# Tokens kept once, in bf16, inside the residual rows; the last chunk's middle gelu tiles in the probabilities' buffer

## The chip, the cores and the metric

The kernel runs on one core of a Trainium2 chip. Five engines work beside each other and meet at semaphores: TensorE (PE, with its weight loads PEld), VectorE (DVE), ScalarE (ACT), GpSimd (POOL) and SyncE (SP, which here only issues DMAs). The metric is the device time of one execution in microseconds; times are medians of several runs.

## The reference

Two layers, each an attention block with a window of 256 tokens and an MLP, over 2048 tokens of width 576. Inputs, weights and output are bf16; both layers use the same weights.

```
def A(x):                       # 32 heads of 18
    q, k, v = (x @ wqkv)        # each [32, 2048, 18]
    s = q @ k.T * 18 ** -0.5    # where 0 <= i - j < 256, else -1e9
    return softmax(s) @ v @ wo
def B(x):
    return gelu(layernorm(x) @ w1 + b1) @ w2 + b2     # 576 -> 4608 -> 576

for layer in range(2):
    x = x + A(layernorm(x))
    x = x + B(layernorm(x))
```

## The kernel before

**Tiles and chunks.** The 2048 tokens are 16 tiles of 128, handled in chunks of four tiles. There are 8 chunks: 0 to 3 are layer one, 4 to 7 layer two (`CH`, `NK`). The residual `x_res` stays in SBUF as float32, one row of 576 per token and tile.

**The stages of a chunk k.** `qkv` (L807, for the first two chunks L767) makes q, k and v; q and k go through `qn` and a DMA transpose (L847) into `qT` and `kT`. `E` is attention, 8 groups of four heads in three parts, `ea`, `eb`, `ec`. In it `scores` (L874) makes the scores of one unit, ACT takes exponentials into `pT` (L883), POOL masks the edges of the window (L904), and `pv` (L921) multiplies with v. DVE normalises (L932 to L942). `tail` (stage `t`) multiplies with wo (L767), adds to the residual (`resid`, L981), takes statistics, and writes the normalised tile through a DMA transpose (L731) into `xnTm`. The MLP goes in three thirds of 12 hidden tiles: `G_part` (stages `ga`, `gb`, `gc`; L1027, 108 matmuls) with gelu on ACT (L1036) into `hT`, and `mm2` (stages `ma`, `mb`, `mc`; L1064, 96 matmuls) with w2, added to the residual, or in the last third of layer two to the output rows (L984).

**One buffer for all thirds.** `hT` holds one third, so the first gelu of a third waits until the product of the third before has read it. In the middle of the kernel the attention of the next chunk stands between the two. For the last chunk there is no next chunk, and the order is G, product, G, product, G, product. The product's first unit of six matmuls reads gelu tiles 0 to 5, all others read all 12. The gelu tiles of a third come in the order 0, 3, 1, 4, 2, 5, 6, 9, 7, 10, 8, 11 (`PAIRS`).

**Where the tokens lie.** Tiles 0 to 11 come in bf16 into the space of w2 (`x_in = w2_sb`), which is free then; the layer norms of chunks 0 to 2 and the first residual add of chunk 0 read them there. The first two w2 loads wait for gelu tiles of chunk 0 for that reason (`gate`). Tiles 4 to 15 are loaded by POOL with a cast to float32 into `x_res` (`x_load`). Parts of `x_res` that are not yet needed hold the transposed q (`qx`) and k (`kx`) of chunk 1.

**What sets the order.** Each step is given to `PL.add` with its engine, what it reads and writes, a cost and a priority. `PL.schedule` then plans all steps with these costs and writes a fixed order for each engine; steps wait for each other by semaphores (`Sched.add`). `PL.nudge` shifts the priority by stage; its numbers were searched for. `Bank` objects get one of the eight PSUM banks when the planner places them: attention scores take three pairs (0, 2, 4), `mm2` takes 7, 6, 5 or 4 (`FILL`), `G_part` any. Filler matmuls (L669) are put into gaps in the first 140 us of the plan. TensorE's array is used in four shapes: full, two halves of 64 rows (L807, L1027), four strips of 32 rows (L874) and four strips of 32 columns (L921).

**The queues.** All weight loads, token loads and transposes are issued by SP, in the planned order; POOL's queue has the three casting loads.

Of the kernel before, what the change touches and what calls it, by code (L numbers as in the profile page):

```python
# [40 lines left out]
class Sched:  # L41
# [23 lines left out]
    def add(self, eng, fn, reads=(), writes=(), dma=None, ring=4, own=False):  # L65
# [11 lines left out]
        for w in writes:  # L77
            for rd in self.readers.get(w, ()):
                if rd[2] != eng or rd[3]:
                    want(rd[:3])  # L80
            lw = self.last_write.get(w)
            if lw is not None and (own or not (eng == "pe" and lw[2] == "pe")):
                want(lw)
# [334 lines left out]
def build_kernel(nc, A_x, A_wqkv, A_wo, B_x, B_w1, B_b1, B_w2, B_b2, out):  # L418
# [42 lines left out]
    PL.nudge = {"": -172.82, "b": -56.78, "ea0.0": 8.44, "ea0.2": 25.12, "ea0.p0": 0.04, "ea0.p1": 10.45, "ea0.p2": -176.5,  # L461
# [120 lines left out]

    x_dram = A_x[0]
    out_dram = out[0]
    x_in = w2_sb

    def mm_cost(n):
        return max(n / 2400.0, 0.026) + (0.003 if n > 64 else 0.0)
# [670 lines left out]
```

## Time and profile before

| what | us |
|---|---|
| median of 3 runs | 888.36 (888.0 to 889.36) |
| the profiled execution | 886.86 |
| its span in the profile | 885.1 |
| PE, ACT, DVE, POOL busy | 860.2, 594.3, 418.8, 369.4 |
| granted TensorE clock | 1.00 |

The profile is one execution. Busy time is that of an engine's instructions, without what only waits or issues DMAs. A wait in a timeline stands in brackets behind the instruction before which the engine was idle, with what ended it. The timelines merge equal instructions that follow each other. Tile names have lost their digits: `w_sb` is `w1_sb` or `w2_sb`, so `w_sb<-in_A_x_dram` are the bf16 tokens. `q2.1`, `ga0` and the like are stages of the plan and appear in no profile.

### The profile page before, as it was taken

To read this page: it belongs to the slowest core of one execution; us is meant where nothing else is said; L and a number is where in the kernel's file an instruction comes from. 1 tells how busy PE (TensorE), PEld (TensorE's weight loads), DVE (VectorE), ACT (ScalarE), POOL (GpSimd) and SP (SyncE) were. 2 spreads that over 40 slices of the span, in tenths; PEclk is the share of its full clock that TensorE was granted. 3 is DMA by queue.
4 is the path that set the end of the run, shared out by engine and by line. 5 is a ranking of instruction groups with operands and counts; after the bars stand their busy time and mean duration, and the time that the engine had idled before them with its cause. 6 is when DMAs were issued, how large, how long until landed. Compare 5 with 4: busy or idle time off the path is not lost.

```text
span 885.1 us, 23132 instructions
## 1 busy us (share of the span) xinstructions
PE 860.2 (97%) x9679; PEld 508.5 (57%) x9679; DVE 418.8 (47%) x994; ACT 594.3 (67%) x741; POOL 369.4 (42%) x503
## 2 busy tenths in 40 slices
PE   9888999999999999999999999999999899999998
PEld 7445555555565556665566655555556455556655
DVE  6889324684337543763347632374325533262111
ACT  5874797778748596466772869747686769853332
POOL 3775464375235561325431446416344356222000
PEclk9999999999999999999999999999999999999999
DMA  7698625852493523864448342595435743347330
GB/s 191 125 191 162 181 89 156 231 129 73 161 177 104 161 83 117 180 150 147 108 126 182 68 161 84 142 191 115 137 123 147 166 138 110 117 124 208 129 119 30
DMA packets 182903, 122.48 MB, mean 138 GB/s; under 512 B 107472, under 2 KB 181264, under 8 KB 182800
## 3 DMA queue, kind: packets, MB, share of 16 engines
q1 hardware_dynamic: 181216, 117.46, 50.9%
q0 software_dynamic: 1584, 3.54, 1.4%
q8 instruction: 77, 1.26, 0.6%
q14 instruction: 26, 0.21, 0.1%
HBM read 91.28 MB, written 2.36 MB: 106 GB/s over the span
## 4 chain that ended last, share of the span: by engine, by line
PE 81%; DVE 4%; POOL 4%; DMA 3%; ACT 3%; issue 3%; SPq 1%; ACTq 0%; DVEq 0%; POOLq 0%
PE ps L1027 31%; PE ps L1064 29%; PE ps L807 7%; PE ps L874 5%; PE ps L921 4%; PE ps L767 4%; POOL pT L904 3%; ACT pT L883 2%; ACT hT L1036 1%; DVE xn L707 1%; DMA xnTm<-xn 1%; DMA xnTa<-xn 1%; DVE xn L715 1%; DVE st_all L682 1%; SPq L614 1%
## 5 line engine op out<-in xcount | busy, mean ns | idle before, releaser
L904 POOL TENSOR_SCALAR_AFFINE_SELECT pT<-pT 128x512 bf16<-128x512 bf16 (+1 forms) x368 | 286.8, 804 | 258.4 <-ACT pT L883 255.2
L883 ACT ACTIVATE pT<-ps 128x1024 bf16<-128x1024 f32 (+2 forms) x384 | 346.2, 972 | 54.1 <-PE ps L874 53.5
L1036 ACT ACTIVATE hT<-ps,b1col 128x512 bf16<-128x512 f32 x288 | 175.2, 688 | 213.0 <-PE ps L1027 212.7
L1064 PE MATMUL ps<-w_sb,hT 128*128 128x288 bf16 x2304 | 309.6, 287 | 3.3 <-ACT hT L1036 2.6
L1027 PE MATMUL ps<-xnTm,w_sb 64*128 64x512 bf16 x2592 | 291.4, 376 | 0.9 <-DMA xnTm<-xn 0.5
L1064 PEld LDWEIGHTS ps<-w_sb,hT 128*128 128x128 bf16 x2304 | 212.7, 98 | 86.0 <-issue 22.8
L1027 PEld LDWEIGHTS ps<-xnTm,w_sb 64*128 64x128 bf16 x2592 | 127.3, 94 | 143.5 <-issue 7.2
L981 DVE TENSOR_TENSOR x_res<-ps,x_res 128x288 f32<-128x288 f32 x216 | 95.6, 446 | 160.8 <-PE ps L1064 140.5
L932 DVE STREAM_TRANSPOSE oq<-ps 128x512 f32<-128x512 f32 x64 | 45.7, 714 | 134.9 <-PE ps L921 134.7
L807 PE MATMUL ps<-wqkv,xnTa 64*128 64x288 bf16 x1296 | 93.7, 283 | 4.2 <-DMA xnTa<-xn 2.0
L828 DVE CAST qn<-ps 128x288 bf16<-128x288 f32 x120 | 49.4, 449 | 79.2 <-PE ps L807 72.6
L807 PEld LDWEIGHTS ps<-wqkv,xnTa 64*128 64x128 bf16 x1296 | 60.4, 94 | 36.0 <-issue 4.5
L874 PE MATMUL ps<-qT,kT 32*128 32x384 bf16 (+2 forms) x1216 | 64.0, 276 | 4.1 <-ACT pT L883 3.7
L695 POOL TENSOR_SCALAR vtmp<-mv_all 128x1 f32<-128x1 f32 (+1 forms) x43 | 8.6, 201 | 133.6 <-DVE mv_all L686 132.4
L1042 POOL TENSOR_TENSOR x_res<-x_res,b2bc 128x576 f32<-128x576 f32 x32 | 40.4, 1283 | 51.8 <-ACT hT L1036 51.7
L921 PE MATMUL ps<-pT,vA 128*20 128x384 bf16 (+2 forms) x1408 | 50.7, 276 | 2.0 <-POOL pT L904 1.5
L874 PEld LDWEIGHTS ps<-qT,kT 32*128 32x128 bf16 x1216 | 19.4, 92 | 45.0 <-issue 28.1
L682 DVE BATCH_NORM_STATS2 st_all<-x_res 128x6 f32<-128x288 f32 x104 | 44.0, 441 | 0.8
L767 PE MATMUL ps<-wo_sb,attT 128*128 128x288 bf16 x320 | 42.1, 286 | 0.7 <-DVE x_res L981 0.6
L815 DVE CAST vA<-ps 128x288 bf16<-128x288 f32 x64 | 26.7, 451 | 34.1 <-PE ps L807 32.0
L707 DVE TENSOR_SCALAR xn<-x_res,mv_all,rstd 128x576 bf16<-128x576 f32 x52 | 36.1, 695 | 9.6 <-DMA xnTm<-xn 5.7
L921 PEld LDWEIGHTS ps<-pT,vA 128*20 128x20 bf16 x1408 | 25.6, 90 | 24.5 <-issue 12.1
(49 smaller groups left out, 388.6 us busy)
## 6 DMA issues: line engine op xcount, KB each, us to landing
w_sb<-in_B_w_dram SPq DMA_DIRECT2D x48, 864.0 KB, 5.7
w_sb<-in_B_w_dram SPq DMA_DIRECT2D x48, 768.0 KB, 4.7
w_sb<-in_B_w_dram SPq DMA_DIRECT2D x96, 48.0 KB, 4.4
x_res<-in_A_x_dram POOLq DMA_DIRECT2D x3, 1152.0 KB, 6.4
out_dram<-xn SPq DMA_DIRECT2D x16, 144.0 KB, 2.0
wqkv<-in_A_wqkv_dram SPq DMA_DIRECT2D x3, 576.0 KB, 5.3
w_sb<-in_A_x_dram SPq DMA_DIRECT2D x2, 576.0 KB, 4.8
wo_sb<-in_A_wo_dram SPq DMA_DIRECT2D x4, 144.0 KB, 2.9
```

The costliest lines, as they stand in the source:

```text
L682: add("dve", lambda e, i=i, s=s: e.bn_stats(st_all[:, t, i, :], s[:, t, i * HB:(i + 1) * HB]), reads=res, writes=[f"st{t}_{i}"], cost=0.37 ...
L767: ins = e.matmul(bank(bs[o])[:, 0:HB], lhs(c), rhs(c, o * HB), start=(c == 0), stop=(c == KD - 1))
L807: ins = e.matmul(bank(bs[o])[:, 0:HB], xnTa[r:r + 64, c, i * 128:(i + 1) * 128], wqkv[r:r + 64, c, col:col + HB], start=(c == 4), stop=(ph ...
L828: add("dve", lambda e, b=bs[o], dst=dst: e.tensor_copy(dst, heads_of(bank(b))), reads=[bs[o]], writes=[f"qn{sl}h{o}"], cost=0.375, lat=0.1 ...
L874: ins = e.matmul(two(bs[j // 2])[:, j % 2, col:col + nq * 128], k_of(T0 + so)[0][32 * j:32 * j + 32, g, :], qs[32 * j:32 * j + 32, g, qo * ...
L883: add("act", lambda e, h2=h2: e.activation(pT[:, sl, 2 * h2:2 * h2 + 2, lo:hi], two(bs[h2])[:, :, lo:hi], ACT.Exp, scale=SCALE), reads=[bs ...
L904: add("pool", lambda e, ap=ap, pat=pat, sgn=sgn, kind=kind: e.affine_select(ap, ap, pattern=pat, compare_op=(ALU.is_ge if kind == "d" else ...
L921: ins = e.matmul(bank(bo)[32 * j:32 * j + VW, qo * 128:(qo + nq) * 128], vA[:, (T0 + so) % VS, 8 * j + g, :], pT[:, sl, j, col:col + nq * ...
L981: add("dve", lambda e: e.tensor_tensor(x_res[:, t, sl], bank(b)[:, 0:HB], x_old[:, t, sl], ALU.add), reads=[b] + ([f"xin{t}"] if first els ...
L1027: ins = e.matmul(bank(bks[i])[:, 0:n], w1_sb[r:r + 64, sls[i], col:col + 128], xnTm[r:r + 64, k % 2, c, 0:n], start=(c == 4), stop=(ph == ...
L1036: add("act", lambda e, ff=ff, fl=fl, bk=bk: e.activation(hT[:, fl, 0:n], bank(bk)[:, 0:n], ACT.Gelu_apprx_tanh, bias=b1col[:, ff:ff + 1]), ...
L1064: ins = e.matmul(bank(b)[:, 0:HB], hT[:, fl, i * 128:(i + 1) * 128], w2_sb[:, fl, hh * HB:(hh + 1) * HB], start=(fl == 0), stop=(fl == NFH ...
```

## The change

1. The tokens are loaded once, in bf16, by SP. `x_in` is now the upper half of the float32 row itself: columns 288 to 575 of `x_res`, seen as 576 bf16 values. Tiles 12 to 15 have a load of their own, and POOL's casting loads are gone. All of layer one's first residual adds, statistics and first layer norms read these bf16 tokens. The add of the upper half (`hh == 1`) overwrites them, so it waits for DVE's own earlier reads of the same row (`own`).
2. The first two w2 loads no longer need the tokens' space: they wait for the first chunk's attention groups 5 and 7 (`aq5`, `aq7`) in place of gelu tiles 0 and 6.
3. `qx` moves into the lower halves of `x_res` rows 8 to 15, `kx` into `xnTm`.
4. The last chunk's middle third writes its gelu tiles into `pT` (`h_of`), which is free after its attention.
5. In the last chunk `mm2` may take any bank not held by `G_part`, and the units of its first two tiles that use gelu tiles 0 to 5 no longer wait for 6 to 11.
6. All numbers of `PL.nudge` are new.

```
-                if rd[2] != eng or rd[3]:
+                if own or rd[2] != eng or rd[3]:
...
-    PL.nudge = {"": -172.82, "b": -56.78, "ea0.0": 8.44, "ea0.2": 25.12, "ea0.p0": 0.04, "ea0.p1": 10.45, "ea0.p2": -176.5,
+    PL.nudge = {"": -255.24, "b": -219.8, "ea0.0": 23.65, "ea0.1": -0.79, "ea0.2": 6.45, "ea0.p0": -38.42, "ea0.p1": 20.22,
...
-    x_in = w2_sb
+    low = x_res[:, :, 0:HB].bitcast(BF16)
+    x_in = x_res[:, :, HB:D].bitcast(BF16)
...
-    qx = x_res[:, 12:16, :].rearrange("p t d -> p (t d)").bitcast(BF16)[:, 0:G * 512].rearrange("p (g c) -> p g c", g=G)
-    kx = x_res[:, 8:12, :].rearrange("p t d -> p (t d)").bitcast(BF16)[:, 0:2 * G * 128].rearrange("p (s g c) -> p s g c", s=2, g=G)
+    qx = low[:, 8:16, 0:512]
+    kx = xnTm[:, 1, 0:4, :].rearrange("p c (a q) -> p (c a) q", a=4).rearrange("p (s g) q -> p s g q", s=2)
...
-    def x_load(a, cnt, reads, prio):
-
-        dma("pool", x_res[:, a:a + cnt, :], x_dram[a * P:(a + cnt) * P, :].rearrange("(t p) d -> p t d", p=P), reads=reads,
-            writes=[r for t in range(a, a + cnt) for r in X(t)] + {8: ["kx0", "kx1"], 12: [f"qx{i}" for i in range(4)]}.get(a, []), cls="xr", ring=8, cost=1.2, prio=prio)
...
-                reads=[f"h{WB * b}"] if gate else [], writes=[f"w2s{b}"] + [f"xin{WB * b + i}" for i in range(WB if gate else 0)], cls="w2", ring=NFH // WB, cost=0.55, lat=2.0, move=0.44 * WB,
+                reads=[gate[b]] if gate else [], writes=[f"w2s{b}"], cls="w2", ring=NFH // WB, cost=0.55, lat=2.0, move=0.44 * WB,
...
+            over = []
+            if first:
+                over = [f"xin{t}"] if hh else [f"qx{i}" for i in range(4)] if t >= 8 else []
             add("dve", lambda e: e.tensor_tensor(x_res[:, t, sl], bank(b)[:, 0:HB], x_old[:, t, sl], ALU.add),
-                reads=[b] + ([f"xin{t}"] if first else []), writes=[f"x{t}h{hh}"], cost=0.375, lat=0.14, prio=prio)
+                reads=[b] + ([f"xin{t}"] if first else []), writes=[f"x{t}h{hh}"] + over, cost=0.375, lat=0.14, prio=prio, own=first and hh == 1)
...
-                resid(t, o, bs[o], prio, first=(k == 0))
+                resid(t, o, bs[o], prio, first=(l == 0))
...
+    hP = pT.rearrange("p s j c -> p (s j) c")
+
+    def h_of(k, hf, fl):
+        if k == NK - 1 and hf == 1:
+            return hP[:, fl, :], f"hp{fl}"
+        return hT[:, fl, :], f"h{fl}"
...
-                b = Bank(FILL)
+                b = Bank(FILL if k < NK - 1 else FILL + (3, 2, 1, 0))
...
-                    add("pe", fn, reads=[f"h{fl}" for fl in range(f0, f0 + 6 if f0 or i + hh == 0 else NFH)] + [f"w2s{f0 // WB}"], writes=[b],
+                    add("pe", fn, reads=[h_of(k, hf, fl)[1] for fl in range(f0, f0 + 6 if f0 or i + hh == 0 or k == NK - 1 and i < 2 else NFH)] + [f"w2s{f0 // WB}"], writes=[b],
...
-            ln_norm_T(t, i, xnTa, "xa", prio, dup=True)
+            ln_norm_T(t, i, xnTa, "xa", prio, None if l else x_in, None if l else [f"xin{t}"], dup=True)
...
-            ln_stats(t, 4 * k - 5)
+            ln_stats(t, 4 * k - 5, x_in, [f"xin{t}"])
...
-            w2_load(0, 1, True)
+            w2_load(0, 1, ("aq5", "aq7"))
...
-                x_load(CH[1][1], CH[1][2], ["aq7"], 0)
+                xin_load(12, 4, ["aq7"], 0)
```

More of the change, by code (lines that the diff above doesn't have):

```diff
@@ L731, in ln_norm_T @@
         add("sp", lambda e: e.dma_start_transpose(dst[:, :, i * 128:(i + 1) * 128], xn[:, sl, :]),
-            reads=rd, writes=[f"{dname}{i}"], dma="t", ring=8, cost=1.3, lat=0.6, move=0.72, desc=640, prio=prio)
+            reads=rd, writes=[f"{dname}{i}"] + (["kx0", "kx1"] if dname == "xm1_" else []), dma="t", ring=8, cost=1.3, lat=0.6, move=0.72, desc=640, prio=prio)
     w1n = [0]
@@ L750, in w1_load, with w2_load @@
                 lat=1.4, move=0.17, desc=64, prio=prio)
-    def w2_load(hf, prio, gate=False):
+    def w2_load(hf, prio, gate=None):
         for b in range(NFH // WB):
@@ L1032, in G_part @@
                         lat=0.22, alloc=(bb if ph == 0 else ()), fifo="pa", own=(ph == 1),
-                        after=([f"h{fs[i] - f}" for i in ix] if ph == 0 else ()))
+                        after=([h_of(k, hf, fs[i] - f)[1] for i in ix] if ph == 0 else ()))
             for ff, bk in zip(fs, bks):
                 fl = ff - f
-                add("act", lambda e, ff=ff, fl=fl, bk=bk: e.activation(hT[:, fl, 0:n], bank(bk)[:, 0:n], ACT.Gelu_apprx_tanh,
+                hd, hn = h_of(k, hf, fl)
+                add("act", lambda e, ff=ff, hd=hd, bk=bk: e.activation(hd[:, 0:n], bank(bk)[:, 0:n], ACT.Gelu_apprx_tanh,
                                                                       bias=b1col[:, ff:ff + 1]),
-                    reads=[bk, "b1"], writes=[f"h{fl}"], cost=0.145 + n * 0.00087, lat=0.17,
+                    reads=[bk, "b1"], writes=[hn] + ([f"p{fl // 4}{x}" for x in ("h0", "h1", "m0", "m1", "m2")] if hn[1] == "p" else []), cost=0.145 + n * 0.00087, lat=0.17,
                     fifo="act", prio=prio)
@@ L1063, in fn @@
                         for fl in range(f0, f0 + 6):
-                            ins = e.matmul(bank(b)[:, 0:HB], hT[:, fl, i * 128:(i + 1) * 128], w2_sb[:, fl, hh * HB:(hh + 1) * HB],
+                            ins = e.matmul(bank(b)[:, 0:HB], h_of(k, hf, fl)[0][:, i * 128:(i + 1) * 128], w2_sb[:, fl, hh * HB:(hh + 1) * HB],
                                            start=(fl == 0), stop=(fl == NFH - 1))
                         return ins
-                    add("pe", fn, reads=[f"h{fl}" for fl in range(f0, f0 + 6 if f0 or i + hh == 0 else NFH)] + [f"w2s{f0 // WB}"], writes=[b],
+                    add("pe", fn, reads=[h_of(k, hf, fl)[1] for fl in range(f0, f0 + 6 if f0 or i + hh == 0 or k == NK - 1 and i < 2 else NFH)] + [f"w2s{f0 // WB}"], writes=[b],
                         cost=6 * mm_cost(HB), lat=0.22, prio=prio + 0.05 * i, alloc=((b,) if f0 == 0 else ()),
@@ L1182, in build_kernel @@
                 w1_load(-1, ["aq6"])
-                x_load(CH[1][1], CH[1][2], ["aq7"], 0)
+                xin_load(12, 4, ["aq7"], 0)
             if k == 1:
                 for n, kk in enumerate(later):
-                    x_load(CH[kk][1], CH[kk][2], [], b + 2)
                     if kk > 2:
```

144 rows, old and new, of the table add are left out of this document.

## The prediction

> **What bounds the kernel now.** I read the page first: its head, the busy time and the chain that ended last.
>
> ```profile
> span 885.1 us, 23132 instructions
> PE 860.2 (97%) x9679; PEld 508.5 (57%) x9679; DVE 418.8 (47%) x994; ACT 594.3 (67%) x741; POOL 369.4 (42%) x503
> ...
> PE 81%; DVE 4%; POOL 4%; DMA 3%; ACT 3%; issue 3%; SPq 1%; ACTq 0%; DVEq 0%; POOLq 0%
> ```
>
> TensorE is busy for 860.2 of 885.1 us and makes up 81% of the chain; no other engine comes above 67%. So an edit can win in two ways only: fewer or cheaper steps on TensorE, or shorter waits of TensorE, of which there are 885.1 - 860.2 = 24.9 us. Then I asked where these lie, by windows: the first attention stage up to 57 us, the stretch up to the first gelu stage, the steady middle, and the last chunk's MLP.
>
> ```profile
> 0.00:57.00 57.00, 49.39 (x524) 31.17 (x524) 43.28 (x112) 42.22 (x63) 33.72 (x60) 1.00 0.72 166
> 57.00:93.40 36.40, 32.59 (x463) 18.84 (x461) 31.92 (x78) 19.98 (x23) 20.99 (x31) 1.00 0.76 153
> 93.40:820.00 726.60, 718.56 (x8195) 420.56 (x8196) 332.66 (x782) 509.54 (x625) 314.67 (x414) 1.00 0.53 140
> 820.00:885.10 65.10, 59.62 (x504) 37.94 (x503) 10.99 (x24) 22.53 (x32) 0.00 (x0) 1.00 0.28 92
> ```
>
> The columns are the stretch, its length, and the busy time of PE, PEld, DVE, ACT and POOL, then the granted clock, the DMA share and GB/s. The clock is 1.00 throughout, so it is no term. TensorE stands still for 7.6, 3.8, 8.0 and 5.5 us. What it waits for in the middle, from the table of waits of that window:
>
> ```profile
> PE ps L807 <- DMA xnTa<-xn: 2.0, 2, 1.4
> PE ps L874 <- ACT pT L883: 1.7, 2, 1.2
> PE ps L921 <- POOL pT L904: 0.7, 1, 0.7
> ...
> PE ps L1027 <- DMA xnTm<-xn: 0.5, 1, 0.5
> ```
>
> Few waits, each at another place: they come from the order in which the planner put the steps. The end is different, as the timeline of PE shows:
>
> ```profile
> 795.29 0.79 PE L767 MATMUL ps<-wo_sb,attT 128*128 128x288 bf16 x5
> 795.91 0.90 PE L1064 MATMUL ps<-w_sb,hT 128*128 128x288 bf16 x6
> 797.01 11.20 PE L1064 MATMUL ps<-w_sb,hT 128*128 128x288 bf16 x90 [0.20 <-ACT hT L1036]
> ...
> 844.52 0.91 PE L1064 MATMUL ps<-w_sb,hT 128*128 128x288 bf16 x6
> 846.25 11.20 PE L1064 MATMUL ps<-w_sb,hT 128*128 128x288 bf16 x90 [0.82 <-ACT hT L1036]
> ```
>
> After the last gelu matmul of a third, the second product can take six matmuls and then waits for the third's last gelu. From 844.52 to 846.25 are 1.73 us, where six matmuls at 0.123 (worked out below) take 0.74: 0.99 lost. The same view has it at 819.90 and 869.14 too; a view of L1064 alone gives the sum over this window:
>
> ```profile
> L1064 PE MATMUL ps<-w_sb,hT 128*128 128x288 bf16 x288 | 36.3, 286 | 2.4 <-ACT hT L1036 2.4
> ```
>
> **The change, part by part.** The sum is against the profiled execution: 886.86 us, span 885.1.
>
> *The last chunk's middle third in the probabilities' buffer.* With its gelu output elsewhere, the first 36 matmuls of that third can run before the second product of the first third. In the changed program's order they do. The relaxed reads and the extra banks let the other two products start with three units of six matmuls (2.2 us) that need only gelu tiles 0 to 5. The need is read from the rows: where six matmuls stand (0.74 us plus one change of shape, 0.83) the gap is 0.82, so 1.65; at 795.29, with five matmuls of L767 in front (0.62 more), the gap is 0.20, so again 1.65. All three covers of the last chunk now exceed 1.65 (4.1, 2.3, 2.3), so 3 x 0.99 = -3.0. But the output projection that stood at 795.29 is moved forward in the new order, so that place falls back to 0.83: from 0.20 to 0.82, +0.6. Term: **-2.4**. The new tiles' weights: the second product's halves are reloaded once the first product has read them, and 72 gelu matmuls lie in between. Below are the page's row of these loads and of the casting token loads, and the chain's row of 108 gelu matmuls:
>
> ```profile
> w_sb<-in_B_w_dram SPq DMA_DIRECT2D x48, 864.0 KB, 5.7
> ...
> x_res<-in_A_x_dram POOLq DMA_DIRECT2D x3, 1152.0 KB, 6.4
> ...
> 93.35 11.83 PE ps L1027 x108
> ```
>
> 72 of 108 are 7.9 us, and such a load lands 5.7 us (median) after its issue: covered; without that cover the loss would be its 5.7 us.
>
> *The retuned order.* The planner's offsets are all new, so every engine's order changes. On TensorE the matmuls are the same except for the fillers. Changes between the array's four shapes (full, 64 rows, 32 rows, 32 columns) go from 499 to 518 in the two programs' orders. One change costs:
>
> ```profile
> 106.21 3.85 PE L1064 MATMUL ps<-w_sb,hT 128*128 128x288 bf16 x30
> 109.99 0.34 PE L874 MATMUL ps<-x_res 32*128 32x384 bf16 x4
> ...
> 110.32 1.64 PE L1064 MATMUL ps<-w_sb,hT 128*128 128x288 bf16 x12
> 111.89 0.40 PE L874 MATMUL ps<-x_res,kT 32*128 32x256 bf16 x8
> ```
>
> Thirty matmuls and one change take 3.78 us from start to start, twelve and one change 1.57, so a matmul is 0.123 and a change 1.57 - 12 x 0.123 = 0.095. 19 x 0.095 = **+1.8**. The fillers go from 50 to 46:
>
> ```profile
> L669 PE MATMUL ps<-warm 128*128 128x256 bf16 x50 | 7.6, 291 | 0.0
> ```
>
> I take 4 x 0.11 (256 columns at the rate above) = **-0.4**.
>
> *Scores that wait for exponentials.* A score step needs banks that the exponentials of the step before free:
>
> ```profile
> 701.00 0.40 PE L874 MATMUL ps<-qT,kT 32*128 32x384 bf16 x8
> 702.62 0.40 PE L874 MATMUL ps<-qT,kT 32*128 32x256 bf16 x8 [1.22 <-ACT pT L883]
> ...
> 704.36 0.40 PE L874 MATMUL ps<-qT,kT 32*128 32x384 bf16 x8 [0.50 <-ACT pT L883]
> ...
> 707.38 0.83 PE L921 MATMUL ps<-pT,vA 128*20 128x384 bf16 x24 [0.71 <-POOL pT L904]
> ```
>
> This is the last chunk's attention: two score steps stand there back to back, then with one unit between them, and 1.22 + 0.50 + 0.71 = 2.4 us go. In the changed order every pair has at least two units (1.6 us) between them at that place. One new thin place, with one unit, is in the first chunk of the second layer, worth about its like here, 0.5, and a few are slightly thinner, 0.5 together. Term: **-1.4** (ends: -2.4, 0).
>
> *The start.* Tokens come in bf16 from SP, the three casting loads by POOL go (POOL is idle there and none waits for it), and 54 more of the third chunk's q, k and v matmuls stand ahead of the first output projection, in the gaps of the first attention stage. TensorE's gaps from 57 us on are the 3.8 us above; before 57 us its order is nearly unchanged. Their evictions are casts on DVE:
>
> ```profile
> L828 DVE CAST qn<-ps 128x288 bf16<-128x288 f32 x120 | 49.4, 449 | 79.2 <-PE ps L807 72.6 <-PE ps L767 6.5
> ```
>
> Eight of them, 3.6 us, now come ahead of the first attention's end, and DVE is busy for 31.9 of these 36.4 us, so I take a third of the gaps: **-1.2** (ends: -3.8, and +2.5 by the chain that ends the stretch). That chain in the timeline, DVE and then SP:
>
> ```profile
> 80.40 0.45 DVE L981 TENSOR_TENSOR x_res<-ps,w_sb 128x288 f32<-128x288 f32 x1
> ...
> 89.22 1.20 SPq L731 DMA_TRANSPOSE xnTm<-xn  x1
> ...
> DMA to landing us min/median/max: 2.5/2.6/6.4
> ```
>
> From the last tile's first residual add to its transpose 8.8 us pass, and it lands 2.6 later: 11.4 us, 1.5 before the gelu matmuls start at 93.35. The new order leaves 8.9 us of TensorE work behind that add. But it has 5.4 us of DVE work in this chain where the old one has 8.0, which makes 11.4 - 2.6 = 8.8 us: even. If the chain stayed at 11.4, 2.5 us would be lost.
>
> *Transposes of the later chunks.* The three waits for them above (2.5 us) lie at places that the new order changes. It has other places where a transposed tile is issued close before its use. I take 0, ends -2.5 and +3.0 (three more like them).
>
> *Sources in bf16, and DVE's waits for itself.* The layer-1 normalisations now all read bf16, and the adds of its residual read bf16 tokens:
>
> ```profile
> L707 DVE TENSOR_SCALAR xn<-x_res,mv_all,rstd 128x576 bf16<-128x576 f32 x52 | 36.1, 695 | 9.6 <-DMA xnTm<-xn 5.7 <-POOL rstd L697 1.9 <-DVE mv_all L686 1.0
> L707 DVE TENSOR_SCALAR xn<-w_sb,mv_all,rstd 128x576 bf16<-128x576 bf16 x12 | 8.1, 675 | 1.7 <-POOL rstd L697 1.6
> L938 DVE TENSOR_TENSOR attq<-oq,rinv 128x288 bf16<-128x288 f32 x64 | 34.5, 538 | 1.2
> ```
>
> Four normalisations (tiles 12 to 15) change their source, 4 x 0.02 us, nothing. The 16 second-half adds that overwrite the tokens wait for the add before them; the nearest row is L938, which reads what DVE has just written: 1.2 us idle over 64. So 0.3 us on an engine that is 47% busy: 0, and 0.3 if its slack were gone.
>
> Sum: -2.4 + 1.8 - 0.4 - 1.4 - 1.2 = **-3.6**, so 883.3 us for the profiled execution. This one is 1.5 us under the median of the runs shown, 888.36; I carry the difference over: **884.8 us**.
>
> **The rivals.**
>
> *No gain (the new order gives it back).* The order's better covers come with 19 changes of shape. If start and score covers bring 0 and two new waits of 0.6 appear, as between other pairs in the middle window, the sum is -2.4 + 1.8 - 0.4 + 1.2 = +0.2: 888.6. For it: the middle window had 8 us of waits though its order was planned too. Against it: the last chunk's 3.0 us hang on no tuning.
>
> *Slower: the second product's first weights in the start's DMA.* Two loads of 864 KB that waited for the first gelu tiles (after 93 us, DMA share 0.53) now go out during the first attention stage, with the last token load, on the queue of the transposes, where the share is 0.76. The transposes there:
>
> ```profile
> L847 SPq DMA_TRANSPOSE kT<-qn x26: 1232/1270/3842, 36.5 to 685.1; - x26
> ...
> DMA to landing us min/median/max: 3.0/3.4/8.3
> ```
>
> If each of the two loads pushes one awaited transpose from the median to the maximum, 2 x 4.9 = +9.8 us, and the time is 884.8 + 9.8 = 894.6. It decides from 3.6 us of such waits. Against it: the casting load that goes took 6.4 us to land in the same stretch. In the Trainium skill (DMA: Bandwidth & Descriptors, Issuing engines are not separate DMA queues) the DMAs of all issuing engines run interleaved on the same 16 engines. By that rule POOL's load frees its 1152 KB alone, and 2 x 864 + 576 KB come: 1152 KB more, the 6.4 us that the casting load took, and 884.8 + 6.4 = 891.2 if all of it is waited for. Which it is the trace of before can't say; its DMA share of 0.76 leaves 8.7 of the 36.4 us free, which speaks for less.
>
> *Faster still.* The start takes all its 3.8 us, the scores their 2.4 and the transposes their 2.5: 884.8 - 2.6 - 1.0 - 2.5 = 878.7.
>
> **How the numbers follow.** A median of three runs tells differences from about 0.2% here (1.8 us): faster is below 886.6, slower above 890.1. My forecast has 0.68 (its own range 881 to 886.6), faster still 0.08, no gain 0.12 and the DMA rival, the longer chain of the start with it, 0.12. Faster is 0.68 + 0.08 = 0.76, the same 0.12, slower 0.12. The range holds the forecast, the nearer half of faster still and nearly all of no gain: 880.5 to 889.6; the DMA rival and the rest of faster still, 0.16, are left out.
>
> **What would show it.** Right: L1064's wait for ACT in the last 65 us falls from 2.4 to under 0.3, while one of about 0.8 stands at the last but one chunk's last product; the last chunk's score steps show no wait over 0.5; the rows of POOL's x_res loads are gone; the busy time of PE rises by about 1.4 us (1.8 - 0.4). Wrong: waits of L807, L874 or L1027 for transposes in the first 95 us above 3.8 us in all, or new waits in the middle above 8.0.

## The result and the profile after

| | before | after |
|---|---|---|
| median of 4 runs, us | 888.77 (888.0 to 889.36) | 881.12 (879.99 to 883.93) |
| ratio, 95% interval | | 0.9919 (0.9894 to 0.9944) |
| profiled execution, us | 886.86 | 880.89 |
| its span | 885.1 | 879.2 |

The change made the kernel faster: the interval of the ratio lies below 1. The medians differ by 7.65 us (0.9%), the profiled executions by 5.97. The head of the page of after:

```profile
span 879.2 us, 23104 instructions
PE 861.2 (98%) x9675; PEld 507.4 (58%) x9675; DVE 414.2 (47%) x994; ACT 596.3 (68%) x741; POOL 367.8 (42%) x500
```

TensorE is busy 1.0 us longer than before (861.2 against 860.2) and waits 6.9 us less (18.0 against 24.9). So the gain is all in waits. The windows of after (the columns are those of the prediction; the last stretch ends at 879.2 here):

```profile
0.00:57.00 57.00, 50.46 (x546) 32.03 (x546) 44.38 (x116) 41.33 (x61) 33.00 (x59) 1.00 0.76 172
57.00:93.40 36.40, 33.97 (x452) 17.96 (x453) 32.32 (x83) 24.51 (x28) 23.09 (x34) 1.00 0.90 183
93.40:820.00 726.60, 720.43 (x8209) 420.64 (x8206) 326.52 (x772) 510.12 (x625) 311.67 (x408) 1.00 0.51 134
820.00:885.10 65.10, 56.31 (x478) 36.82 (x474) 10.99 (x24) 20.31 (x29) 0.00 (x0) 1.00 0.25 86
```

In the first three stretches the idle time of TensorE falls from 7.6, 3.8 and 8.0 to 6.5, 2.4 and 6.2 us. The DMA share of the second rises from 0.76 to 0.90, as the rival of the first w2 loads had it. The end, in the timeline of PE of after:

```profile
792.51 0.91 PE L1071 MATMUL ps<-w_sb,hT 128*128 128x288 bf16 x6
794.23 11.20 PE L1071 MATMUL ps<-w_sb,hT 128*128 128x288 bf16 x90 [0.82 <-ACT hT L1043]
805.36 15.71 PE L1033 MATMUL ps<-xnTm,w_sb 64*128 64x512 bf16 x144
821.01 11.93 PE L1071 MATMUL ps<-w_sb,hT 128*128 128x288 bf16 x96
832.87 7.94 PE L1033 MATMUL ps<-xnTm,w_sb 64*128 64x512 bf16 x72
840.75 11.93 PE L1071 MATMUL ps<-w_sb,pT 128*128 128x288 bf16 x96
852.62 11.83 PE L1033 MATMUL ps<-xnTm,w_sb 64*128 64x512 bf16 x108
864.38 11.93 PE L1071 MATMUL ps<-w_sb,hT 128*128 128x288 bf16 x96
```

The three waits of 0.8 in the last chunk are gone: its last matmul now ends 864.38 + 11.93 - 805.36 = 70.95 us after its first. In before the first and the last row of this stretch, in the timeline, are

```profile
808.14 11.83 PE L1027 MATMUL ps<-xnTm,w_sb 64*128 64x512 bf16 x108
...
870.86 11.20 PE L1064 MATMUL ps<-w_sb,hT 128*128 128x288 bf16 x90 [0.81 <-ACT hT L1036]
```

That is 870.86 + 11.20 - 808.14 = 73.92 us, so 2.97 less now. The expectations below use two other ends of this stretch: the last instruction of any engine (71.45 us, in before 74.41) and the end of the span (73.8, in before 77.0). At 794.23 the new wait of 0.82 stands where before had 0.20. What TensorE waits for in the middle of after (93.4 to 820 us), from the table of waits:

```profile
PE ps L1071 <- DVE x_res L980: 2.0, 3, 0.9
PE ps L1071 <- DVE oq L928: 1.1, 1, 1.1
PE ps L803 <- DMA xnTa<-xn: 0.9, 1, 0.9
PE ps L1071 <- ACT hT L1043: 0.8, 1, 0.8
PE ps L803 <- DVE x_res L980: 0.8, 1, 0.8
```

In this window no score step waits for exponentials any more and no product with v for the mask (1.7 and 0.7 us in before), and the waits for transposed tiles fall from 2.5 to 0.9. Waits for DVE take part of it back. The start, in the timeline of after:

```profile
50.59 0.79 PE L763 MATMUL ps<-wqkv,xnTa 128*128 128x288 bf16 x5 [0.33 <-DVE qn L824]
...
77.63 0.79 PE L763 MATMUL ps<-wo_sb,attT 128*128 128x288 bf16 x5 [0.57 <-DVE x_res L980]
...
89.80 6.43 PE L1033 MATMUL ps<-xnTm,w_sb 64*128 64x512 bf16 x56
```

The first gelu matmul stands at 89.80, in before at 93.35: 3.55 earlier. The waits of TensorE ahead of it fall by 2.5 us, and 1.1 us of its work moved behind it. From there to the last chunk's first gelu matmul it takes 715.6 us, before 714.8: the moved work and the changes of shape, less waits. With the last stretch taken to the end of the span (73.8 against 77.0, so -3.1), the sum is -3.55 + 0.8 - 3.1 = -5.9.

### The profile page after: what moved, and what is told of

It is laid out like the page before. It is cut to its first block, busy times and chain, and to the rows that moved or that the text cites. A ratio compares the mean times of both kernels' runs of the same rounds, so it can differ in the third digit from the quotient of the medians.

```text
span 879.2 us, 23104 instructions
## 1 busy us (share of the span) xinstructions
PE 861.2 (98%) x9675; PEld 507.4 (58%) x9675; DVE 414.2 (47%) x994; ACT 596.3 (68%) x741; POOL 367.8 (42%) x500
## 3 DMA queue, kind: packets, MB, share of 16 engines
q8 instruction: 77, 1.26, 0.6%
## 4 chain that ended last, share of the span: by engine, by line
PE 80%; DVE 7%; DMA 4%; ACT 4%; issue 3%; POOL 2%; SPq 0%; DVEq 0%; POOLq 0%
PE ps L1033 31%; PE ps L1071 28%; PE ps L803 9%; PE ps L870 5%; PE ps L917 4%; PE ps L763 4%; ACT pT L879 3%; DVE xn L703 2%; DMA xnTm<-xn 2%; POOL pT L900 1%; DVE st_all L678 1%; DVE xn L711 1%; DMA xnTa<-xn 1%; DVE x_res L980 1%; ACT hT L1043 1%
## 5 line engine op out<-in xcount | busy, mean ns | idle before, releaser
L1071 PE MATMUL ps<-w_sb,hT 128*128 128x288 bf16 x2208 | 298.5, 287 | 3.8 <-DVE x_res L980 2.0
L1043 ACT ACTIVATE hT<-ps,b1col 128x512 bf16<-128x512 f32 x276 | 168.4, 688 | 195.3 <-PE ps L1033 194.6
L1071 PEld LDWEIGHTS ps<-w_sb,hT 128*128 128x128 bf16 x2208 | 203.2, 98 | 84.6 <-issue 23.7
L980 DVE TENSOR_TENSOR x_res<-ps,x_res 128x288 f32<-128x288 f32 x224 | 99.1, 446 | 170.1 <-PE ps L1071 136.3
L678 DVE BATCH_NORM_STATS2 st_all<-x_res 128x6 f32<-128x288 f32 (+1 forms) x128 | 53.7, 443 | 1.7 <-DMA x_res<-in_A_x_dram 1.2
L703 DVE TENSOR_SCALAR xn<-x_res,mv_all,rstd 128x576 bf16<-128x576 f32 (+1 forms) x64 | 43.8, 685 | 13.8 <-DMA xnTm<-xn 5.7
L763 PE MATMUL ps<-wo_sb,attT 128*128 128x288 bf16 x320 | 44.2, 287 | 0.6 <-DVE x_res L980 0.6
```

The lines of the kernel that those rows point to most:

```text
L678: add("dve", lambda e, i=i, s=s: e.bn_stats(st_all[:, t, i, :], s[:, t, i * HB:(i + 1) * HB]), reads=res, writes=[f"st{t}_{i}"], cost=0.37 ...
L703: add("dve", lambda e: e.tensor_scalar(xn[:, sl, 0:D], s[:, t, :], mv_all[:, t, 0:1], rstd[:, t:t + 1], op0=ALU.subtract, op1=ALU.mult), r ...
L763: ins = e.matmul(bank(bs[o])[:, 0:HB], lhs(c), rhs(c, o * HB), start=(c == 0), stop=(c == KD - 1))
L980: add("dve", lambda e: e.tensor_tensor(x_res[:, t, sl], bank(b)[:, 0:HB], x_old[:, t, sl], ALU.add), reads=[b] + ([f"xin{t}"] if first els ...
L1043: add("act", lambda e, ff=ff, hd=hd, bk=bk: e.activation(hd[:, 0:n], bank(bk)[:, 0:n], ACT.Gelu_apprx_tanh, bias=b1col[:, ff:ff + 1]), rea ...
L1071: ins = e.matmul(bank(b)[:, 0:HB], h_of(k, hf, fl)[0][:, i * 128:(i + 1) * 128], w2_sb[:, fl, hh * HB:(hh + 1) * HB], start=(fl == 0), sto ...
```

## The experiments

### The last chunk

*The kernel before with points 4 and 5 of the change and the new offsets for the last chunk's MLP stages alone (`tail_all2`), and the same without point 4 (`tail_reads2`).*

```
-                b = Bank(FILL)
+                b = Bank(FILL if k < NK - 1 else FILL + (3, 2, 1, 0))
...
-  f0 + 6 if f0 or i + hh == 0 else NFH
+  f0 + 6 if f0 or i + hh == 0 or k == NK - 1 and i < 2 else NFH
...
+        if k == NK - 1 and hf == 1:                # tail_all2 alone
+            return hP[:, fl, :], f"hp{fl}"
```

> The kernel before with points 4 and 5 of the change alone, and the new offsets for the last chunk's MLP stages alone; the order up to the last chunk's first second product is that of before. Theory of the covers: the stretch from the last chunk's first gelu matmul to the end falls from 76.96 us in the trace of before to 73.9 (3 x 0.99 = 3.0 us less, two more changes of array shape 0.2), L1064's waits for gelu tiles in it go from 2.4 to under 0.3, and the time is 3.0 us under the kernel before. Rival, the weights come too late once the products stand closer together: a wait for the w2 loads takes the place of the gelu wait, and the stretch stays within 1 us of 76.96.

> As the run with points 4 and 5, but without the gelu tiles in the probabilities' buffer: only the relaxed reads and the extra banks of the last chunk's products. Theory of the covers: three units of 2.3 us in all stand before the first that needs the last gelu tile, more than the 1.65 needed, so the whole 3.0 us come without the buffer: stretch 73.9, L1064's waits for gelu tiles under 0.3. Rival, the buffer is what removes the waits: at least one of the three 0.8 us waits stays, stretch 74.9 to 77.

Measured: `tail_all2` 886.75 us, ratio 0.9966 (0.9946 to 0.9985); `tail_reads2` 885.95, ratio 0.9969 (0.9947 to 0.9991). The timeline of `tail_reads2` has first and last row of the last chunk's MLP as

```profile
809.28 11.83 PE L955 MATMUL ps<-xnTm,w_sb 64*128 64x512 bf16 x108
...
868.29 11.93 PE L992 MATMUL ps<-w_sb,hT 128*128 128x288 bf16 x96
```

with no wait between: 70.94 us, the 70.95 of after, and 71.44 to the end of the last engine. `tail_all2` has 71.45. To the end of the span both take 74.0 us, where 73.9 was expected, and in the total the ratios make 3.0 and 2.8 us. So the 3.0 us come without the buffer: from the relaxed reads, the extra banks and the few offsets of these stages, which were not tested one by one. The probabilities' buffer, which lets 36 gelu matmuls go ahead, adds nothing here: with three units of six matmuls that need only gelu tiles 0 to 5 the cover of 2.2 us already exceeds the 1.65 that is needed.

*The kernel before with points 4 and 5 and its own offsets (`tail_all`).* The planner then puts the last third's first product ahead of the middle third's second product.

> The kernel before with its own offsets, the last chunk's middle third in the probabilities' buffer, the relaxed reads and the extra banks. With these offsets all 180 remaining gelu matmuls stand ahead of the second product of the middle third, and the last product follows it with nothing between. Theory (a second product's weights land 5.6 us after the issue, and the issue waits for the reads of the half before, 0.74 before the product's end): TensorE waits 4 to 6 us for the load there, no wait for gelu tiles is left, and from the last chunk's first gelu matmul to the end it takes 71.45 + 4.9 = 76.3, more than before's 74.41. Rival (with the DMA nearly idle at the end a load lands sooner, or the planner's distance is enough): under 2 us, 71.5 to 73.5.

Measured: 890.33 us in one run. The timeline, and a window of it:

```profile
808.87 15.71 PE L1034 MATMUL ps<-xnTm,w_sb 64*128 64x512 bf16 x144
...
871.87 13.56 PE L1072 MATMUL ps<-w_sb,hT 128*128 128x288 bf16 x96 [4.02 <-DMA w_sb<-in_B_w_dram]
```

```profile
871.80:874.00 2.20, 2.13 (x9) 1.34 (x10) 0.00 (x0) 0.00 (x0) 0.00 (x0) 0.50 0.87 314
```

The wait for the weights is 4.02 us, within the 4 to 6 expected, and no wait for gelu is left. What was not expected: behind the wait the granted clock is 0.50, and the last 96 matmuls take 13.56 us in place of 11.93. So the place costs 4.02 + 1.63 = 5.65 us, and the stretch to the end of the last engine is 77.05. The prediction had put the loss without this cover at 5.7: about right in sum, but made up otherwise, so the agreement is luck.

*The changed kernel with the relaxed reads and the banks also for the last product of the last chunk but one (`after_mc6`).*

```
-  b = Bank(FILL if k < NK - 1 else FILL + (3, 2, 1, 0))
+  b = Bank(FILL if k < NK - 1 and (k, hf) != (NK - 2, 2) else FILL + (3, 2, 1, 0))
...
-  ... or k == NK - 1 and i < 2 else NFH
+  ... or (k == NK - 1 or k == NK - 2 and hf == 2) and i < 2 else NFH
```

> The changed kernel, with the relaxed reads and the extra banks also for the last product of the last chunk but one, where the trace of after shows 0.82 us of waiting for a gelu tile behind six matmuls. Theory (a cover of 1.65 us is needed there, as in the last chunk): with two units of six matmuls in front, 1.57, the wait at 794 falls from 0.82 to under 0.15 and the time from 881.1 to about 880.4. Rival (the wait hangs on ScalarE's late start there, not on what TensorE has to do meanwhile): ScalarE's gelu ends later by as much, 0.5 or more of the wait stays, and the time does not change.

Measured: 881.14 us, ratio 0.9904 (0.9886 to 0.9922). The product of that place, in the timeline, now runs on without a wait behind its first six matmuls:

```profile
795.77 12.19 PE L1071 MATMUL ps<-w_sb,hT 128*128 128x288 bf16 x96
```

From the first gelu matmul to the last chunk's first it takes 713.9 us, against 714.4 to 715.6 in five kernels with after's order (after, `after_cast`, `shape_full`, `shape_part`, `after_w2late`; mean 714.8). So the wait of 0.82 is gone and the middle is shorter by about as much. The total does not show it: 0.8 us is 0.1%, less than the intervals. The runs can't tell this kernel and after apart.

### The start

All kernels with one start share a point: the five matmuls of L767 (L763 in after) with 0.33 us of waiting ahead of them, at 51.28 in before and 50.59 in after. When it comes varies by some 2 us from execution to execution. The time from it to the first gelu matmul hardly does: 42.07, 42.16, 42.22 and 42.02 with before's start (before, `tail_reads2`, `tail_all2`, `tail_all`), 39.21, 39.39 and 39.34 with after's (after, `shape_full`, `shape_part`). This measure is used below; between the two starts it falls by 2.8 us.

One trace is left out of this: that of `after_mc6`, whose start is that of after, takes 43.08. From 74 to 77 us its DMA engines counted as busy (share 1.33) but moved 39 GB/s, the last column, where those of after moved 292, and the token load issued at 69.84 landed 7.4 us later, in place of 5.2 to 5.6 in after, `shape_full`, `shape_part` and `after_w2late`. The residual adds came late by this, the output projections waited 1.80 and 0.65 us, and the clock was halved behind them.

```profile
74.00:77.00 3.00, 2.72 (x34) 1.42 (x28) 0.69 (x3) 2.49 (x3) 2.54 (x5) 1.00 1.33 39
79.30:86.10 6.80, 6.09 (x45) 2.47 (x44) 5.07 (x14) 1.94 (x2) 4.42 (x8) 0.50 0.46 99
```

What held the DMA engines in this execution is not known. Its trace shows that a single measure of a start can be off by more than the differences read below, so each is read together with the wait that makes it.

*The code of before with all new offsets (`before_newn`), and the code of after with the old offsets for the stages of the start (`after_oldstart`).* The edit is `PL.nudge` alone.

> The kernel before with all new offsets: tokens loaded twice, casting loads and late w2 loads as before, no change in the last chunk's buffer. Its order up to the first gelu matmul is nearly that of the changed kernel. If the start's gain is the order (the third chunk's q, k and v matmuls in the gaps of the first attention stage), the first gelu matmul starts at 90.0 +- 0.7 us (93.35 before, 89.80 after) and the time is 2 to 4 us under before, short of the changed kernel by the 3 us of the last chunk. If it is the casting load that no longer stands before the transposes, it starts at 92.5 to 94 and the time is within 1.5 us of before.

> The changed kernel with the old offsets for the stages of the start alone (chunks 0 and 1 up to the first gelu stage, and the third chunk's q, k and v). Its order there is nearly that of before, the tokens come as in the changed kernel. If the start's gain is the order, the first gelu matmul starts at 92.5 to 94 us and the time is 2 to 4 us over the changed kernel. If it is the casting load, it starts at 90 to 91.3 (at least the 1.3 us wait at 74 us gone and more).

Measured: `before_newn` 894.02 us, ratio 1.0053 (1.0035 to 1.0071); `after_oldstart` 918.92, ratio 1.0315 (1.0271 to 1.0359). From the timeline, the table of waits of the middle and a window of `before_newn`:

```profile
50.31 0.79 PE L767 MATMUL ps<-wqkv,xnTa 128*128 128x288 bf16 x5 [0.34 <-DVE qn L828]
...
90.52 5.79 PE L1027 MATMUL ps<-xnTm,w_sb 64*128 64x512 bf16 x52
```

```profile
PE ps L874 <- ACT pT L883: 5.7, 10, 1.1
```

```profile
755.20:758.60 3.40, 3.40 (x24) 1.21 (x18) 0.82 (x2) 3.38 (x4) 3.14 (x5) 0.50 0.70 252
```

The start is 40.21 long with the casting loads still in it, so the new order takes 1.9 of the 2.8 us by itself. From the shared point on, TensorE idles 2.2 us here, 4.5 in before and 2.6 in after. So the order alone takes out the waits. The 0.9 us that are left to after's start are no wait, but 1.4 us less work, 14 matmuls (ten of q, k and v, four fillers), with 0.4 us more of waiting. But the middle gets 9.9 us longer than in before (724.7 against 714.8; 6.1 longer than in the slowest of four traces with before's order): ten score steps wait for exponentials, 5.7 us, and for 3.4 us the clock is halved. The expected gain in the total did not come. `after_oldstart` loses in the start (first gelu matmul at 96.60) and far more behind it, where the clock is halved too (0.987 to 0.993 on average over its four runs); its table of waits from 95 to 820 us begins

```profile
PE ps L798 <- ACT pT L807: 13.1, 14, 3.1
```

The offsets and the code fit only each other: a priority changed in the start moves banks and slots of all later steps in the plan. Halves of the two can't be read as halves of the gain.

*The changed kernel with one surplus casting load in the start (`after_cast`).*

```
                 xin_load(12, 4, ["aq7"], 0)
+                hf32 = hT.rearrange("p f c -> p (f c)").bitcast(FP32)[:, 0:4 * D].rearrange("p (t d) -> p t d", t=4)
+                dma("pool", hf32, x_dram[4 * P:8 * P, :]..., reads=["aq7"], writes=[f"h{f}" for f in range(9)], ...)
```

> The changed kernel, with one of the casting loads put back at its old place in the start (1152 KB as POOL moves it, float32 tokens of the second chunk, into gelu space that nothing needs yet); no instruction of the five engines but POOL's one issue moves. Left out: nothing, the load is only surplus. Theory (the start was shortened by its order, the loads' traffic was hidden): the first gelu matmul stays at 89.8, within 0.5, and the time within 0.2% of the changed kernel's 881.1. Rival (the casting loads held up the start's DMA): transposes in the start land later, the first gelu matmul comes at 91 to 93 and the time rises by 1 to 3 us.

Measured: 884.49 us, ratio 0.9943 (0.9923 to 0.9964). The timeline:

```profile
51.33 0.79 PE L763 MATMUL ps<-wqkv,xnTa 128*128 128x288 bf16 x5 [0.33 <-DVE qn L824]
...
78.72 0.79 PE L763 MATMUL ps<-wo_sb,attT 128*128 128x288 bf16 x5 [1.55 <-DVE x_res L980]
80.15 0.79 PE L763 MATMUL ps<-wo_sb,attT 128*128 128x288 bf16 x5 [0.65 <-DVE x_res L980]
...
91.94 4.35 PE L1033 MATMUL ps<-xnTm,w_sb 64*128 64x512 bf16 x38
```

40.61 us, 1.3 more than the 39.3 of after's start, and the median is 3.4 us above after's (2.1 by the ratios to before, whose intervals just overlap; the profiled execution 1.7: 882.62 against 880.89). The first output projections wait 2.2 us for the residual adds where after waits 0.57. `after_mc6` has such waits too, but there the DMA engines hardly moved anything at that time; here they did. That window of `after_cast`, then the row of DVE behind which those adds stand, in after and in `after_cast`:

```profile
74.00:77.00 3.00, 3.00 (x44) 1.73 (x36) 1.14 (x4) 2.31 (x3) 2.57 (x6) 1.00 1.55 315
```

```profile
74.63 0.82 DVE L678 BATCH_NORM_STATS2 st_all<-x_res 128x6 f32<-128x288 bf16 x2 [0.32 <-DMA x_res<-in_A_x_dram]
```

```profile
77.48 0.82 DVE L678 BATCH_NORM_STATS2 st_all<-x_res 128x6 f32<-128x288 bf16 x2 [2.35 <-DMA x_res<-in_A_x_dram]
```

DVE takes its steps in the planned order and waits there for the last token load, of 576 KB. It lands 7.5 us after its issue in place of 5.2, with the surplus load under way beside it (issued at 69.71, landed 11.4 us later). So the theory that the loads' traffic was hidden falls, and the rival has it: it had put the first gelu matmul at 91 to 93. What TensorE waits for in the end is the token load, which the change itself put there, and not a transpose.

*The kernel before with that casting load moved out of the start (`before_cast0`).*

```
-                x_load(CH[1][1], CH[1][2], ["aq7"], 0)
+                dma("pool", x_res[:, 4:8, 0:2], ..., reads=["aq7"], ...)     # 4 KB
...
             w2_load(0, 1, True)
+            dma("pool", x_res[:, 4:8, :], ..., reads=["h0"], ...)            # the load itself
```

> The kernel before, with the second chunk's casting load out of the start: its place there keeps a load of 4 KB, and the load itself is issued behind the first gelu tile. Every engine's order but POOL's is that of before. Counted from a point that both share (the five matmuls of L767 at 51.28 in the trace of before, with 0.33 us of waiting ahead of them) the first gelu matmul comes 42.07 us later in before, 42.16 and 42.22 in two kernels with its start. Theory (the surplus casting load cost 1.3 us in the changed order, so it cost something here too): 41.0 to 41.6. Rival (in before's order there was room for the load, the 1.3 us came of three loads in one place): 42.0 to 42.2. Either way the start does not reach the changed kernel's 39.3, which comes of the order.

Measured: 892.88 us, ratio 1.0039 (1.002 to 1.0059). First the step of TensorE that waits in before, and the issue table's row for the `kT` transpose that SP issues at 68.29 there (its last number is the time from issue to landing); then the rows of `before_cast0` that answer to them, where that transpose is issued at 67.83:

```profile
74.10 0.34 PE L874 MATMUL ps<-x_res 32*128 32x384 bf16 x4 [1.32 <-issue]
74.26 0.24 PE L874 MATMUL ps<-x_res,kT 32*128 32x128 bf16 x4
```

```profile
kT<-qn SPq DMA_TRANSPOSE x1, 5.7
```

```profile
50.82 0.79 PE L767 MATMUL ps<-wqkv,xnTa 128*128 128x288 bf16 x5 [0.33 <-DVE qn L828]
...
72.25 0.34 PE L874 MATMUL ps<-x_res 32*128 32x384 bf16 x4
...
91.52 5.79 PE L1027 MATMUL ps<-xnTm,w_sb 64*128 64x512 bf16 x52
```

```profile
kT<-qn SPq DMA_TRANSPOSE x1, 3.3
```

40.70 us, 1.4 less than before's 42.1 and a little under the 41.0 to 41.6 of the theory. This is the mechanism in before's order: POOL's load is issued at 66.65 and takes 6.4 us to land. The `kT` transpose issued into that time lands 5.7 us after its issue, at 74.0, in place of 3.3, and the score step at 74.10, whose second half reads this `kT`, starts 1.32 us late. The profile names no releaser for this wait ("issue"); that it is this transpose follows from the times, and from three more traces with before's start (`tail_reads2`, `tail_all2`, `tail_all`), where it lands 5.7 to 5.9 us after its issue and the same step waits 1.42, 1.48 and 1.26 us. Without the load the wait is gone. That agrees with the Trainium skill (DMA: Bandwidth & Descriptors, Issuing engines are not separate DMA queues), by which the DMAs of POOL and SP interleave on the same engines. In `before_newn` the wait is gone too, though the load is there: the last `kT` transpose of the stretch is issued at 66.61, ahead of the load at 68.77, and no step waits for it.

The total rises all the same. The load now stands behind the first gelu tile, where another is awaited; a row of the timeline there:

```profile
109.23 1.64 PE L1064 MATMUL ps<-w_sb,hT 128*128 128x288 bf16 x12 [2.47 <-DMA w_sb<-in_B_w_dram]
```

Before waits for no w2 load there. The mean granted clock is below 1.00 in 7 of the 10 runs, and in 3 of the 13 of before beside them, so how much of the rise is this wait is not known. The move alone does not pay; what it would bring to drop the load in before's order, no run shows.

*The changed kernel with the first two w2 loads moved out of the start (`after_w2late`).*

```
-            w2_load(0, 1, ("aq5", "aq7"))
+            # per half: 3 KB at its old place, the load itself with reads=[f"h{b}"]
```

> The changed kernel, with the second product's first two loads of 864 KB out of the start: their places there keep loads of 3 KB, and the loads themselves are issued behind the first gelu tiles. TensorE's order is that of the changed kernel but for three fillers ahead of the first gelu matmul (0.33 us). From the shared point (50.59 in the trace of after) to the first gelu matmul it takes 39.21 there, and 39.39 and 39.34 in two other kernels with its start. Theory (order sets the start, these loads are hidden): 39.2 to 39.7. Rival (the loads in the start's DMA cost what the surplus casting load cost, in proportion 1.0 to 2.0 us, so the changed kernel left that much): 37.3 to 38.5.

Measured: 882.08 us, ratio 0.9909 (0.9886 to 0.9933). The timeline:

```profile
52.49 0.79 PE L763 MATMUL ps<-wqkv,xnTa 128*128 128x288 bf16 x5 [0.33 <-DVE qn L824]
...
92.41 4.92 PE L1033 MATMUL ps<-xnTm,w_sb 64*128 64x512 bf16 x44
```

39.92 us, of which 0.33 are the three fillers: 39.59, against 39.3 with the loads. The two loads of 864 KB in the start cost nothing that TensorE waits for, though they raise the DMA share from 0.78 to 0.90 (the same stretch of this kernel and of after). They do slow their neighbours: the `qT` transpose issued behind the second one lands 8.0 us after its issue in after and 6.2 here, but no wait for it shows. The DMA rival is false.

### What a change of shape costs

*The changed kernel with a surplus matmul of 64 columns behind each of the last chunk's 48 units of six, in the full shape (`shape_full`) or in 32 rows (`shape_part`).*

```
+  ins = e.matmul(bank(b)[:, 320:384], h_of(k, hf, fl)[0][0:32, i * 128:(i + 1) * 128],
+                 w2_sb[0:32, fl, 0:64], start=True, stop=True, tile_position=(0, 0), ...)
```

> The changed kernel, with one surplus matmul of 64 columns behind each of the 48 units of six matmuls in the last chunk's MLP, in the full shape of the array, into columns of the bank that nobody reads. It is the control for the same kernel with the matmuls in 32 rows. From the last chunk's first gelu matmul to the end it takes 73.8 us without them; each of them costs between 0.027 (64 of 288 columns at 0.123) and 0.1, so 75 to 79.

> The same 48 surplus matmuls in 32 rows of the array, so with two changes of shape each, 96 in all. Theory (a change costs 0.095 us): the last stretch is 96 x 0.095 = 9.1 us longer than with the full shape. Rival (the 0.095 between unlike matmuls belongs to the score and probability steps where it was read, as their operands or banks, and a change as such costs nothing): under 2 us longer.

Measured: the stretch to the end of the last engine takes 72.85 us in `shape_full` and 82.49 in `shape_part`. To the end of the span `shape_full` takes 75.2, at the lower edge of what was expected. The timelines of `shape_full` and of `shape_part`:

```profile
833.06 0.19 PE L1075 MATMUL ps<-w_sb,hT 128*128 128x64 bf16 x1
...
833.82 0.19 PE L1075 MATMUL ps<-w_sb,hT 128*128 128x64 bf16 x1
```

```profile
834.87 0.20 PE L1075 MATMUL ps<-w_sb,hT 32*128 32x64 bf16 x1
...
835.85 0.20 PE L1075 MATMUL ps<-w_sb,hT 32*128 32x64 bf16 x1
```

From one small matmul to the next are 0.76 us in the full shape and 0.98 in 32 rows. Over the stretch: the 48 matmuls cost 72.85 - 71.45 = 1.40, and the 96 changes 82.49 - 72.85 = 9.64, so 0.100 each. The 0.095 of the prediction was a price of the change as such. That is shown for changes between the full shape and 32 rows. For those between the full shape and 64 rows the rows of after's last chunk give about the same: 144 matmuls take 15.71 us and 72 take 7.94, so one takes 0.108, and from 832.87 to 840.75 are 7.88, 0.11 more than 72 of them. The strips of 32 columns were not priced.

## Why the prediction was right or wrong

The time fell inside the range, 3.7 us under the forecast of 884.8. In the profiled executions the sum was -3.6 and -5.97 came. By its steps:

- *The last chunk, -2.4.* Right in size: -2.97 in the stretch and +0.62 at the last but one chunk's product, -2.35. The need of 1.65 us, read from two gaps, gave the new wait at 794.23 exactly (1.65 - 0.83 = 0.82), and covers of 2.2 us (`tail_reads2`, after) and of 1.57 (`after_mc6`) left no wait. Wrong in one reason: the step gave the probabilities' buffer a part, and it had none. The price of the weights' cover, 5.7, came as 4.02 of waiting and 1.63 of halved clock.
- *The changes of shape, +1.8.* Right in its price: 19 x 0.100 = 1.9, if all kinds of change cost alike. The busy time of PE rose by 1.0, where 1.4 was named; what makes the difference was not traced.
- *Scores that wait for exponentials, -1.4.* Too small: all 2.4 went, and neither the new thin place nor the slightly thinner ones show a wait in after. The far end of its range was right.
- *The start, -1.2.* This is the term that was off: the waits ahead of the first gelu matmul fell by 2.5 us. From 57 us on they fell from 3.8 to 2.4, so by 1.4, near the term; but the third that the step took of these gaps was a guess, and one gap of the 3.8 makes up nearly all of the 1.4. The other 1.1 lie ahead of 57 us, where the step held the order for nearly unchanged and put nothing (0.6 of it ahead of the shared point, where executions differ anyway). Its main idea, that the new order fills the gaps, holds: the order alone brings TensorE's idle time from the shared point on from 4.5 to 2.2 us (`before_newn`). Its second reason was wrong. It took POOL's casting load for free ("POOL is idle there and none waits for it"). No step waits for the load, but TensorE waits for what the load delays: the one gap above is the 1.32 us at 74.10, for a `kT` transpose, and with the load out of the way the start is 1.4 us shorter. What the loads' removal brought in the change itself stays open: the order alone already takes this wait away, and where one load is put back (`after_cast`, 1.3 us) it delays a token load that before does not have. The prediction's row of `kT` transposes could not tell this: it was read as one of the start ("the transposes there"), but covers the whole program: its 3842 ns stand at 685.10, and the landing of 8.3 us belongs to a transpose at 681.71. The one that is awaited in the start held the queue for 1.23 us and landed after 5.7.
- *Transposes of the later chunks, 0.* The waits for them fell by 1.6 us, and waits for DVE's adds and transposes came in their place; all waits of the middle together went from 8.0 to 6.2. Of these -1.9 the scores are -2.4 and the wait at 794.23 is +0.6, so about -0.1 is left for the rest. Zero was no bad value for it, but only as a sum: the single waits all changed.
- *The carry-over to the median* was too small: before's profiled execution lay 1.9 us under its median of 888.77, after's 0.2 under its own. The mean granted clock of a run may give a part of this: it is below 1.00 in 20 of the 47 runs of before that stood beside these kernels, and in 1 of 13 of after, `after_mc6` and `after_w2late`. Before's trace has the longer idle stretches (last section); whether that is why, and how much of the 1.7 us it makes, was not measured.
- *The rivals.* No gain: false, since the waits went down with the new order and not up. The first w2 loads: false, with the loads out of the start it is no shorter. Their premise, that a load slows the transposes beside it, is true of the load that went and of those that came; but beside these stands no transpose that TensorE waits for. They were not tried at other places.

What stays open: why the middle of the same order varies between executions (714.8 to 718.6 in before, `tail_reads2`, `tail_all` and `tail_all2`) beyond the halved clock of 3.4 us in `tail_all2`. Open too is what held the DMA engines in `after_mc6`.

## What to carry to other kernels

When an engine is named idle and its DMA "waited for by none", look at what the transfer does to the transfers beside it: take those issued while it is under way, add to each its time to landing, and see whether a step starts just then. A row that covers the whole program does not tell this. Where a product waits for the last of its producers' tiles, first relax which units wait for which tiles; in the last chunk that gave all that a second buffer gave. An order that was searched for belongs to its code: the two that were tried in other code were slower than either whole.

## What was not expected of the hardware

*Waits shorter than 2.2 us can halve the clock.* Two windows of `tail_all2`:

```profile
200.00:204.10 4.10, 1.99 (x28) 1.06 (x24) 1.58 (x4) 1.26 (x2) 0.00 (x0) 1.00 0.85 246
204.20:207.60 3.40, 3.40 (x26) 1.55 (x21) 0.00 (x0) 0.68 (x2) 0.00 (x0) 0.50 0.00 0
```

In `tail_all2` TensorE idles for 2.1 of 4.1 us; from 204.20 the granted clock is 0.50 for 3.4 us. In `after_mc6` it was 0.50 from 79.3 to 86.1 (the row in the section on the start) behind waits of 1.80 at 78.52 and 0.65 at 79.96, and in `before_newn` for 3.4 us behind a wait of 1.13 at 753.13 with others close by. Over 3.4 us the idle time ahead of these three was 2.1, 2.45 and 1.8 us; but in `after_cast` and `before_cast0` 2.2 and 2.5 us of it went without a drop. The Trainium skill (TensorE: Matmul & The Clock Gate, HAM oscillation — how this bites in real kernels) warns of gaps above about 3.4 us; here less than that was enough in some executions, and the time at half clock, 3.4 or 6.8 us, agrees with windows of that length. Before's largest idle time in 3.4 us is 1.7, after's 1.5.

*One DMA of 1152 KB on POOL's queue delays transposes on SP's*: in before one lands 5.7 us after its issue in place of 3.3, and the next holds SP's queue for 3.21 us in place of 1.26 (`before_cast0`). The second of the two w2 loads, of 864 KB on SP's own queue, delays one too (8.0 against 6.2), but none that was awaited (`after_w2late`).
